# Scanning two sequences at a time in a Mamba-2 scan followed by a cosine-gated MLP

## The chip, the cores and the metric

The kernel runs on one core of one Trainium2 chip. The metric is the device time of one execution in microseconds. The engines of a core work from queues of their own, each in order: PE (TensorE; PEld is its weight load), DVE (VectorE), ACT (ScalarE), POOL (GpSimd), and SP, which here only issues DMAs. They wait for each other through semaphores.

## The reference

Part one is a scan over chunks. For 4 batches, 8 heads, 768 positions, head size 32 and state size 16 it computes, chunk by chunk:

```python
L = exp(cum[i] - cum[j]) * (i >= j)          # products of a from j+1 to i
M = (C @ B.T) * L
y = M @ x  +  (C @ state) * exp(cum)         # inside the chunk, and from the chunks before
state = exp(sum(la)) * state + sum_j(B_j x_j * exp(cum[-1] - cum[j]))
```

Part two takes y as a (3072, 256) matrix: `h = y @ w_in` (256 to 2048), `g = h * cos(h)`, `out = g @ w_out` (2048 to 256). Everything is in fp32.

## The kernel before

The kernel scans chunks of 128 positions, so there are NC = 6 of them; a "sequence" b is one of the 4 batches with all its 8 heads. Part two runs in 96 steps, 16 for each chunk, numbered n. The loop over n at the end of the code sets the order on every engine: the code is written out in the order in which each engine's queue shall hold it, and nothing reorders it.

A step n has these pieces. `first(n)` computes a 128x512 piece of h in PSUM (tile hp, L462; two such banks take turns); ACT rounds it (k, L466), DVE takes the fraction of a turn (w, L468). `gate(n)` lets ACT take the sine (L473, it writes w in place) and DVE multiply it with hp (gT, L475). From chunk 1 on `differ(n)` lets POOL form differences of gT (gd, L500, L502, L503), since `second` there uses seven products in place of eight. `second(n-2)` multiplies gT and gd with w_out, or with sums of its blocks (tile words after `differ_w`, L494), into o (L518 in chunk 0, L556 after it). After every eighth step o is copied out and combined by four POOL additions (sum, L571).

The scan of a sequence of chunks 1 to 5 is spread over four steps in a row. `reaches` and the first half of `decays` come first: scans on DVE which give the running product of a along the chunk (reach, L333) and the decays of four heads (lam, L342). Then `turn` (with the second half of decays): PE transposes B and C into tp (L355, L356), ACT copies them to cT and bcT (L360, L362) and DVE writes C times reach (L364). Then `intra`: four matmuls on strips of 32 rows give g (L374), DVE multiplies it with lam (m, L387). Then `finish`: y is summed from the state (L397) and from m (L406), ACT copies it to yT (L411), `sum_up` gives the chunk's share of the state (s_ps, L423) and `carry` renews the state (whole on DVE, L438, state on POOL, L441). The tiles tp, g, y and s_ps take turns in two PSUM buffers of two banks each ("scan"). Sequences 0 to 3 of a chunk start at the steps 6, 10, 14 and 18 of the chunk before.

In chunk 0 there is one more job. The weights come from DRAM in 16 pieces (words) and are rounded in place: `grade` (ACT L193 and L191, POOL L194) and `join` (DVE L207 and L209, POOL L217). Piece n is graded and joined in step n, the join behind gT. The clipped a is written to DRAM (a_cut, a_all, L637) and read back broadcast over the partitions (arow, along) for the scans.

The loop's end, where the four steps of a sequence stand:

```python
            if j == 0:
                reaches(c, b)
                decays(c, b, 0)
            elif j < 4:
                (turn, intra, finish)[j - 1](c, b)
                if j == 1:
                    decays(c, b, 1)
```

Of the kernel before, what the change touches and what calls it, by code (L numbers as in the profile page):

```python
# [25 lines left out]
def kernel(  # L26
# [50 lines left out]
    states = ctx.enter_context(tc.tile_pool(name="states", bufs=NB + 1))  # L77
# [252 lines left out]
    def reaches(c, b):  # L330

        reach[c, b] = r = scan.tile([P, P], FP32, tag="reach", bufs=2, name="reach")
        V.tensor_tensor_scan(out=r, data0=along[c][:, b], data1=ones, initial=1.0,  # L333
                             op0=ALU.mult, op1=ALU.mult)
# [16 lines left out]
    def turn(c, b, tag=None):  # L351
        bc = raw[c][0]
        tp = (pair("tp")[:, 0] if tag is None else bank([P, 4 * P], "tp", tag)
              ).rearrange("p (k i) -> p k i", k=4)
        PE.transpose(tp[:, 0], bc[:, 0, heads(b)].rearrange("p h n -> p (h n)"), ident)  # L355
        PE.transpose(tp[:, 1], bc[:, 1, heads(b)].rearrange("p h n -> p (h n)"), ident)  # L356
# [4 lines left out]
        bcT = scan.tile([P, 2, P], FP32, tag="bcT", name="bcT")  # L361
        ACT.copy(out=bcT[:, 0], in_=tp[:, 0])  # L362
        if c > 0:
            V.tensor_tensor(out=bcT[:, 1], in0=tp[:, 1], in1=reach[c, b], op=ALU.mult)  # L364
        part[c, b] = (bcT, cT)

    def intra(c, b):
        bcT, cT = part[c, b]
        g = [pair("g") for _ in range(2)]
        for u in range(4):  # L370
            r = slice(32 * u, 32 * u + 32)
            rhs = (cT[r].rearrange("p t i -> p (t i)") if c > 0 else
                   cT[r].rearrange("p t (s i) -> p s t i", s=2))
            PE.matmul(g[u // 2][:, u % 2, 0:2 * P], lhsT=bcT[r, 0], rhs=rhs,  # L374
                      start=True, stop=True)
        l = lam.pop((c, b))
        m = scan.tile([P, H, P] if c > 0 else [P, 2, H, W], FP32, tag="m", name="m")

        def of(t, u):
            hs = slice(u * HH, (u + 1) * HH)  # L380
            return (t[:, hs].rearrange("p (k t) i -> p k (t i)", k=2) if c > 0 else
                    t[:, :, hs].rearrange("p s (k t) i -> p k s (t i)", k=2))
        for u in range(2):
            in0 = g[u][:, :, 0:2 * P]
            if c == 0:
                in0 = in0.rearrange("p k (s i) -> p k s i", s=2)
            V.tensor_tensor(out=of(m, u), in0=in0, in1=of(l, u), op=ALU.mult)  # L387
        part[c, b] = (bcT, m)

    def finish(c, b, tag=None, fills=0):  # L390
        (bcT, m), xr = part.pop((c, b)), raw[c][1]
        if c > 0:

            y = pair("y")[:, :, 0:P]
            for q in range(4):
                r, p = slice(32 * q, 32 * q + 32), 64 * (q % 2)
                PE.matmul(y[p:p + 64, q // 2], lhsT=state[c - 1, b][r].rearrange("p t d -> p (t d)"),  # L397
                          rhs=bcT[r, 1], start=True, stop=False, tile_position=(32 * q, p),
                          skip_group_check=True)
        else:  # L400
            y = bank([P, 4, P], "y", tag)
            fill(y[:, 2:4], fills)
            y = y[:, 0:2]
        for h in range(H):
            q, t = h % 4, h // 4
            PE.matmul(y[32 * q:32 * q + 32, t], lhsT=xr[:, b, h], rhs=m[:, h] if c > 0 else m[:, :, h],  # L406
                      start=(c == 0 and t == 0), stop=True, tile_position=(0, 32 * q),
                      skip_group_check=True)
        if b == 0:
            yT[c] = two.tile([P, 2, TB], FP32, tag="yT", name="yT")  # L410
        ACT.copy(out=yT[c][:, :, b * P:(b + 1) * P], in_=y)  # L411
# [323 lines left out]
```

## Time and profile before

| | |
|---|---|
| median of 3 runs | 397.01 us (396.37 to 397.31) |
| the profiled execution's own time | 395.98 us |
| its span, first to last instruction | 394.2 us |
| PE busy | 385.5 us (98%) |
| DVE, ACT, POOL busy | 258.3, 178.4, 248.5 us (66%, 45%, 63%) |
| mean granted TensorE clock | 0.994 |

The time is the span and 1.8 us around it. The busy share of PE counts matmuls that wait in the array as work, so the 98% does not say that PE runs at its best. The trace counts every matmul as two rows, since it is run in two passes: four matmuls of the code are "x8". Line numbers of the profile are those of the kernel before; those of the changed kernel are named with the changed names.

### The profile page before, as it was taken

To read this page: it belongs to the slowest core of one execution; us is meant where nothing else is said; L and a number is where in the kernel's file an instruction comes from. 1 tells how busy PE (TensorE), PEld (TensorE's weight loads), DVE (VectorE), ACT (ScalarE), POOL (GpSimd) and SP (SyncE) were. 2 spreads that over 40 slices of the span, in tenths; PEclk is the share of its full clock that TensorE was granted. 3 is DMA by queue.
4 is the path that set the end of the run, shared out by engine and by line. 5 is a ranking of instruction groups with operands and counts; after the bars stand their busy time and mean duration, and the time that the engine had idled before them with its cause. 6 is when DMAs were issued, how large, how long until landed. Compare 5 with 4: busy or idle time off the path is not lost.

```text
span 394.2 us, 7794 instructions
## 1 busy us (share of the span) xinstructions
PE 385.5 (98%) x2980; PEld 331.8 (84%) x2980; DVE 258.3 (66%) x408; ACT 178.4 (45%) x343; POOL 248.5 (63%) x373
## 2 busy tenths in 40 slices
PE   8989998999999999999999999999999999999996
PEld 2578876788899898898898998988988989889995
DVE  8877877587666765756756657648557656673443
ACT  4777664443444444344434434333434344444431
POOL 6665566638757657847846846857765755754651
PEclk9999999899999999999999999999999999999999
DMA  7969899709502309702206812122120000010011
GB/s 89 277 176 282 240 212 143 151 21 136 125 2 62 87 2 116 140 2 62 79 10 98 107 51 60 30 62 60 28 62 0 23 6 0 2 29 0 2 28 27
DMA packets 106373, 30.43 MB, mean 77 GB/s; under 512 B 75520, under 2 KB 102240, under 8 KB 106336
## 3 DMA queue, kind: packets, MB, share of 16 engines
q1 hardware_dynamic: 106176, 29.81, 37.2%
q8 instruction: 23, 0.38, 0.4%
q10 hardware_dynamic: 160, 0.13, 0.1%
q14 instruction: 14, 0.11, 0.1%
HBM read 26.59 MB, written 3.34 MB: 76 GB/s over the span
## 4 chain that ended last, share of the span: by engine, by line
PE 84%; DVE 6%; POOL 3%; DMA 2%; ACT 2%; SPq 1%; issue 1%; POOLq 0%; DVEq 0%
PE hp L462 38%; PE o L556 31%; PE g L374 3%; PE y L406 3%; PE y L397 2%; PE o L518 2%; DVE mag L209 2%; DMA words<-in_moe_w_out_dram 1%; DMA arow<-a_cut 1%; POOL w_in L217 1%; DVE mag L207 1%; DVE lam L342 1%; ACT w L473 1%; PE a_ps L298 1%; DVE w L468 1%
## 5 line engine op out<-in xcount | busy, mean ns | idle before, releaser
L462 PE MATMUL hp<-yT,w_in 128*128 128x256 f32 x768 | 187.5, 387 | 0.3 <-POOL w_in L217 0.2
L462 PEld LDWEIGHTS hp<-yT,w_in 128*128 128x128 f32 x768 | 139.5, 191 | 26.0 <-issue 7.4
L500 POOL TENSOR_TENSOR gd<-gT 128x256 f32<-128x256 f32 x79 | 79.7, 1008 | 90.3 <-DVE gT L475 84.6
L475 DVE TENSOR_TENSOR gT<-hp,w 128x512 f32<-128x512 f32 x96 | 66.4, 692 | 81.5 <-ACT w L473 79.4
L473 ACT ACTIVATE w<-w,quarter 128x512 f32<-128x512 f32 x96 | 69.3, 722 | 105.0 <-DVE w L468 105.0
L466 ACT ACTIVATE k<-hp 128x512 int32<-128x512 f32 x96 | 57.4, 598 | 94.0 <-PE hp L462 94.0
L468 DVE SCALAR_TENSOR_TENSOR w<-hp,k 128x512 f32<-128x512 f32 x96 | 65.1, 679 | 43.9 <-ACT k L466 43.9
L556 PE MATMUL o<-words,gd 128*128 128x128 f32 x474 | 65.8, 275 | 0.0
L556 PEld LDWEIGHTS o<-words,gd 128*128 128x128 f32 x474 | 59.3, 192 | 0.0
L342 DVE TENSOR_TENSOR_SCAN lam<-arow,unit 128x512 f32<-128x512 f32 x40 | 56.2, 1404 | 0.0
L556 PEld LDWEIGHTS o<-w_out,gT 128*128 128x128 f32 x316 | 47.6, 191 | 4.0
L502 POOL TENSOR_TENSOR gd<-gT,gd 128x128 f32<-128x128 f32 x79 | 44.7, 566 | 6.2
L556 PE MATMUL o<-w_out,gT 128*128 128x128 f32 x316 | 48.0, 274 | 0.0
L503 POOL TENSOR_TENSOR gd<-gT,gd 128x128 f32<-128x128 f32 x79 | 35.9, 455 | 6.2
L387 DVE TENSOR_TENSOR m<-g,lam 128x512 f32<-128x512 f32 x48 | 30.7, 682 | 1.6 <-PE g L374 0.6
L518 PE MATMUL o<-w_out,gT 128*128 128x256 f32 x128 | 30.8, 384 | 1.0 <-POOL w_out L217 1.0
L556 PE MATMUL o<-words,gT 128*128 128x128 f32 x158 | 30.6, 275 | 0.0
L556 PE MATMUL o<-w_out,gd 128*128 128x128 f32 x158 | 30.5, 275 | 0.0
L518 PEld LDWEIGHTS o<-w_out,gT 128*128 128x128 f32 x128 | 24.7, 194 | 4.9 <-POOL w_out L217 1.4
L556 PEld LDWEIGHTS o<-words,gT 128*128 128x128 f32 x158 | 24.0, 192 | 0.0
L556 PEld LDWEIGHTS o<-w_out,gd 128*128 128x128 f32 x158 | 24.0, 192 | 0.0
L217 POOL TENSOR_TENSOR w_in<-mag,last 128x512 uint32<-128x512 uint32 (+1 forms) x9 | 12.3, 1368 | 13.0 <-DVE mag L209 9.2
(83 smaller groups left out, 308.4 us busy)
## 6 DMA issues: line engine op xcount, KB each, us to landing
arow<-a_cut SPq DMA_DIRECT2D x20, 512.0 KB
words<-in_moe_w_in_dram SPq DMA_DIRECT2D x8, 512.0 KB
words<-in_moe_w_out_dram SPq DMA_DIRECT2D x8, 512.0 KB
out_dram<-sum SPq DMA_DIRECT2D x18, 128.0 KB
xr<-in_x_dram SPq DMA_DIRECT2D x4, 512.0 KB
along<-a_all SPq DMA_DIRECT2D x20, 64.0 KB
xr<-in_x_dram SPq DMA_DIRECT2D x8, 128.0 KB
bc<-in_B_dram SPq DMA_DIRECT2D x4, 256.0 KB
```

The source lines that it names most:

```text
L342: V.tensor_tensor_scan(out=lam[c, b][:, hs].rearrange("p h i -> p (h i)"), data0=rows_.rearrange("p h i -> p (h i)"), data1=unit.rearrange ...
L387: V.tensor_tensor(out=of(m, u), in0=in0, in1=of(l, u), op=ALU.mult)
L462: PE.matmul(to_[:, e], lhsT=w_in[:, k, fs], rhs=y[:, k, u], start=(k == 0), stop=(k == KT - 1), skip_group_check=True)
L466: ACT.activation(k, hp[n], AF.Copy, bias=0.25, scale=INV_2PI)
L468: V.scalar_tensor_tensor(out=w, in0=hp[n], scalar=INV_2PI, in1=k, op0=ALU.mult, op1=ALU.subtract)
L473: ACT.activation(cos, cos, AF.Sin, bias=quarter, scale=TWO_PI)
L475: V.tensor_tensor(out=gT[n], in0=hp.pop(n), in1=cos, op=ALU.mult)
L500: G.tensor_tensor(out=d[:, 0:2], in0=g[:, 1:2].to_broadcast([P, 2, P]), in1=g[:, 3::-3], op=ALU.subtract)
L502: G.tensor_tensor(out=d[:, 2], in0=g[:, 0], in1=d[:, 0], op=ALU.subtract)
L503: G.tensor_tensor(out=d[:, 3], in0=g[:, 2], in1=d[:, 2], op=ALU.subtract)
L518: PE.matmul(o[c, u][:, t], lhsT=g[:, 2 * e + t], rhs=w_out[:, 2 * j + e], start=(j == e == t == 0), stop=(j == NJ - 1 and e == 1), skip_gr ...
L556: PE.matmul(at[q], lhsT=a_[q], rhs=w[q], start=(j == 0 and q in starts), stop=(j == NJ - 1), skip_group_check=True)
```

## The change

In chunks 1 to 5 two sequences (a pair, u = 0 or 1) are scanned together: `turn2` transposes both, `intra2` forms g of both, `masked` multiplies with lam one sequence in each of two steps, and `finish2` sums y from both states, then from both m, then both sums. Pair u starts (`turn2`) at step 11 (u = 0) or 19 (u = 1) for chunk 1, and 16 steps later for each chunk after it; g stands one step later, finish2 three steps later. The four halves of decays stand in the four steps ahead of turn2, one in each, and both reaches in the last of these; for the first pair of chunk 1 the halves stand at the steps 4, 6, 8 and 9. `turn2` stands ahead of the sine in its step.

In chunk 0 a piece is graded one step ahead from step 2 on, and from step 3 on the join stands between w and gT. The differences of w_out are made two at a time at the steps 14, 15, 17 and 19. The clip of a is on POOL for both copies and stands ahead of the first join. One more short matmul on ones stands at the start, the third transpose of chunk 0 stands ahead of the second `cross`, and the buffers of states, sum and reach are changed.

```diff
+    def turn2(c, u):
+        tp = pair("tp")[:, 0].rearrange("p (s k i) -> p s k i", s=2, k=2)
+        for s in range(2):
+            for k in range(2):
+                PE.transpose(tp[:, s, k], bc[:, k, heads(2 * u + s)]..., ident)
+        bT = scan.tile([P, 2, P], FP32, tag="bT2", bufs=1, name="bT2")
+        ACT.copy(out=bT, in_=tp[:, :, 0])
+        cT = scan.tile([P, 2, 2, P], FP32, tag="cT2", bufs=1, name="cT2")
+        for t in range(2):
+            ACT.activation(cT[:, :, t], tp[:, :, 1], AF.Copy, scale=slot[:, t:t + 1])
+        rT = scan.tile([P, 2, P], FP32, tag="rT", bufs=1, name="rT")
+        V.tensor_tensor(out=rT, in0=tp[:, :, 1], in1=reach[c, u], op=ALU.mult)
+    def intra2(c, u):
+        g = [pair("g") for _ in range(2)]
+        for s in range(2):
+            for q in range(4):
+                r = slice(32 * q, 32 * q + 32)
+                PE.matmul(g[q // 2][:, q % 2, s * 2 * P:(s + 1) * 2 * P], lhsT=bT[r, s],
+                          rhs=cT[r, s]..., start=True, stop=True)
...
-    V.tensor_scalar(out=la, in0=a_in, **clip)
     cut = const.tile([RB, NU, P], FP32, name="cut")
     G.tensor_scalar(out=cut, in0=a_in, **clip)
     G.memset(cut[:, :, 0:1], 0.0)
+    G.tensor_scalar(out=la, in0=a_in, **clip)
...
+    join("in", 0)
+    finish(2, "o")
+    intra(3)
...
-    differ_at = {NF - 7: (0, fore), NF - 6: (1, fore), NF - 5: (2, fore), NF - 4: (3, fore),
-                 NF - 1: (0, hind), NF: (1, hind), NF + 1: (2, hind), NF + 2: (3, hind)}
+    differ_at = {NF - 2: [(0, fore), (1, fore)], NF - 1: [(2, fore), (3, fore)],
+                 NF + 1: [(0, hind), (1, hind)], NF + 3: [(2, hind), (3, hind)]}
+    TURN = (NF - 5, NF + 3)
...
+            for at in pairs(n):
+                turn2(*at)
+            rests = [grade(*piece[m], later=True) for m in ... if m in piece]
             gate(n)
...
+            if not early and n in piece:
+                join(*piece[n])
+            gated(n)
...
         if n >= LAG:
             second(n - LAG)
+        for c, u in pairs(n - 1):
+            intra2(c, u)
+            masked(c, 2 * u)
+        for c, u in pairs(n - 2):
+            masked(c, 2 * u + 1)
+        for c, u in pairs(n - 3):
+            finish2(c, u)
+        for c, b, t in halves_at(n):
+            decays(c, b, t)
+        for c, u in pairs(n + 1):
+            for b in (2 * u, 2 * u + 1):
+                reaches(c, b)
```

Three places in the built order. On PE, the scan of sequence 0 of chunk 1, from its transposes to its sums (hp and o are part two). Before:

```order
L355 MATMUL tp<-ident,bc 128x128
L356 MATMUL tp<-ident,bc 128x128
L462 MATMUL hp<-yT,w_in 128x256 x4
L518 MATMUL o<-w_out,gT 128x256 x4
L374 MATMUL g<-cT,bcT 128x256 x4
L462 MATMUL hp<-yT,w_in 128x256 x4
L518 MATMUL o<-w_out,gT 128x256 x4
L397 MATMUL y<-bcT,state 64x128 x4
L406 MATMUL y<-m,xr 32x128 x8
L423 MATMUL s_ps<-xr,sc 32x64 x4
```

The same place now, for sequences 0 and 1:

```order
L405 MATMUL tp<-ident,bc 128x128 x4
L571 MATMUL o<-w_out,gT 128x256 x4
L512 MATMUL hp<-yT,w_in 128x256 x4
L571 MATMUL o<-w_out,gT 128x256 x4
L422 MATMUL g<-cT_724,bT_722 128x256 x8
L512 MATMUL hp<-yT,w_in 128x256 x4
L571 MATMUL o<-w_out,gT 128x256 x4
L512 MATMUL hp<-yT,w_in 128x256 x4
L571 MATMUL o<-w_out,gT 128x256 x4
L447 MATMUL y<-rT,state 64x128 x8
L454 MATMUL y<-m,xr 32x128 x16
L471 MATMUL s_ps<-xr,sc 32x64 x8
```

Each group of the scan holds twice the matmuls, so PE goes from part two to the scan and back half as often; a step more lies between g and y.

On ACT, the turn of sequence 1 of chunk 1 before (w is the sine, mag and last are the grading):

```order
L466 ACTIVATE k<-hp 128x512
L193 ACTIVATE mag<-words 128x512
L473 ACTIVATE w<-w,quarter 128x512
L191 ACTIVATE last<-words 128x512
L360 ACTIVATE cT<-tp,slot 128x128 x2
L362 COPY bcT<-tp 128x128
L466 ACTIVATE k<-hp 128x512
```

The turn of the first pair now:

```order
L516 ACTIVATE k<-hp 128x512
L408 COPY bT_722<-tp 128x256
L411 ACTIVATE cT_724<-tp,slot 128x2x128 x2
L193 ACTIVATE mag<-words 128x512
L523 ACTIVATE w<-w,quarter 128x512
L191 ACTIVATE last<-words 128x512
L516 ACTIVATE k<-hp 128x512
```

The copies of the transposes no longer stand behind the sine.

On DVE, steps of chunk 1 in which the next scans are made. Before:

```order
L468 SCALAR_TENSOR_TENSOR w<-hp,k 128x512
L475 TENSOR_TENSOR gT<-hp,w 128x512
L333 SCALAR_TENSOR_TENSOR reach<-along,ones 128x128
L342 SCALAR_TENSOR_TENSOR lam<-arow,unit 128x512
L468 SCALAR_TENSOR_TENSOR w<-hp,k 128x512
L475 TENSOR_TENSOR gT<-hp,w 128x512
L364 TENSOR_TENSOR bcT<-tp,reach 128x128
L342 SCALAR_TENSOR_TENSOR lam<-arow,unit 128x512
L468 SCALAR_TENSOR_TENSOR w<-hp,k 128x512
L475 TENSOR_TENSOR gT<-hp,w 128x512
L387 TENSOR_TENSOR m<-g,lam 128x512 x2
L468 SCALAR_TENSOR_TENSOR w<-hp,k 128x512
```

Now (ps is the copy of o after every eighth step):

```order
L518 SCALAR_TENSOR_TENSOR w<-hp,k 128x512
L528 TENSOR_TENSOR gT<-hp,w 128x512
L344 SCALAR_TENSOR_TENSOR lam<-arow,unit 128x512
L518 SCALAR_TENSOR_TENSOR w<-hp,k 128x512
L528 TENSOR_TENSOR gT<-hp,w 128x512
L619 COPY ps<-o 128x512
L344 SCALAR_TENSOR_TENSOR lam<-arow,unit 128x512
L518 SCALAR_TENSOR_TENSOR w<-hp,k 128x512
L528 TENSOR_TENSOR gT<-hp,w 128x512
L344 SCALAR_TENSOR_TENSOR lam<-arow,unit 128x512
L335 SCALAR_TENSOR_TENSOR reach<-along,ones 128x128 x2
L518 SCALAR_TENSOR_TENSOR w<-hp,k 128x512
```

The scans of lam, which came in two of every four steps, now come in four steps in a row and then not for four; the copy ps lies among them, and both reaches stand behind the last.

More of the change, by code (lines that the diff above doesn't have):

```diff
@@ L399, in finish @@
                           skip_group_check=True)
[L400 to L409, printed above, removed]
-            yT[c] = two.tile([P, 2, TB], FP32, tag="yT", name="yT")
@@ L411, in finish @@
-        ACT.copy(out=yT[c][:, :, b * P:(b + 1) * P], in_=y)
-        if 0 < c < NC - 1:
-            sum_up(c, b, pair("s_ps")[:, 0, 0:2 * D])
-            carry(c, b)
-    sums = {}
+        for s in range(2):
+            for h in range(H):
+                q, t = h % 4, h // 4
+                PE.matmul(y[32 * q:32 * q + 32, t, s * P:(s + 1) * P], lhsT=xr[:, 2 * u + s, h],
+                          rhs=ms[s][:, h], start=False, stop=True, tile_position=(0, 32 * q),
+                          skip_group_check=True)
@@ L605 @@
     fill(warm, 2)
+    fill(warm[:, 0:2])
     spread_a(0, "h")
-    turn(0, 0)
+    turn(0)
     spread_a(1, "h")
```

215 lines of the change are left out of this document (125 added, 90 removed).

## The prediction, made before the changed kernel was run

> **What bounds the kernel now.** I read the page's chain of work that ended last, then the granted clock and busy time by stretches, then PE's timeline of a steady stretch and of every place where PE stood still.
>
> ```profile
> PE 84%; DVE 6%; POOL 3%; DMA 2%; ACT 2%; SPq 1%; issue 1%; POOLq 0%; DVEq 0%
> ...
> 49.20:65.40 16.20, 15.62 (x102) 12.90 (x98) 12.03 (x19) 7.96 (x14) 11.04 (x12) 1.00 0.97 191
> 68.90:72.30 3.40, 3.40 (x9) 2.69 (x8) 1.40 (x3) 1.83 (x3) 3.15 (x4) 0.50 1.28 168
> 75.00:385.00 310.00, 309.96 (x2493) 276.27 (x2490) 196.77 (x299) 130.82 (x248) 199.56 (x306) 1.00 0.26 48
> ```
>
> The columns of the last three lines are the stretch and its length, busy time of PE, PEld, DVE, ACT and POOL, the granted clock, DMA. From 75 us to 385 PE never stops (309.96 of 310.00); there only what PE itself spends counts, as long as DVE (63%) and POOL (64%) keep up. Before 75 PE has waits, and once the clock is halved for 3.4 us.
>
> What PE spends there on one sequence of the scan (chain first, then timeline; start, length):
>
> ```profile
> 141.24 1.73 PE hp L462 x8
> 142.97 1.56 PE o L556 x14
> ```
>
> ```profile
> 144.36 0.27 PE L355 MATMUL tp<-ident,bc 128*128 128x128 f32 x1
> ...
> 144.58 1.89 PE L462 MATMUL hp<-yT,w_in 128*128 128x256 f32 x8
> 146.31 0.61 PE L556 MATMUL o<-w_out,gT 128*128 128x128 f32 x4
> ...
> 147.97 0.71 PE L374 MATMUL g<-cT,bcT 32*128 32x256 f32 x8
> 148.61 1.99 PE L462 MATMUL hp<-yT,w_in 128*128 128x256 f32 x8
> 150.44 0.61 PE L556 MATMUL o<-w_out,gT 128*128 128x128 f32 x4
> ...
> 152.09 0.45 PE L397 MATMUL y<-bcT,state 32*64 32x128 f32 x8
> 152.47 0.64 PE L406 MATMUL y<-m,xr 128*32 128x128 f32 x16
> 152.93 0.29 PE L423 MATMUL s_ps<-xr,sc 128*32 128x64 f32 x8
> 153.16 0.48 PE L462 MATMUL hp<-yT,w_in 128*128 128x256 f32 x1
> ```
>
> A step of part two is 1.73 + 1.56 = 3.29 us, so 256 columns stream in 1.73 / 8 = 0.216 us. The transposes take 144.58 - 144.36 = 0.22 and cost nothing at either side. The g group: o from 146.31 would be through at 147.87, g starts at 147.97 (0.10 lost), hp follows at 148.61 (0.64), and this hp takes 150.44 - 148.61 = 1.83 where 1.73 is usual (0.10 lost): 0.84 together. Four strips run side by side, so the streaming in it is two passes, 0.43; 0.41 is switching. The y group in the same way: 152.00 to 153.16, and 0.10 in the hp behind: 1.26. Its streams are 0.22 (L397, two passes of 128 columns), 0.43 (L406, four) and 0.11 (L423, two of 64): 0.76. So 0.50 is switching.
>
> **Term 1, the scan in pairs: -9.0 us.** A pair has the streams of two sequences and, if the second sequence's matmuls follow without a gap, the switching of one: it saves 0.41 + 0.50 = 0.9 us. There are 10 pairs (the last two without s_ps, which hardly touches the switching): 9.0. The transposes save nothing. All of it lies on the path where PE never stops; the first pair saves it only if PE is the bound there too (term 2). Bounds: a gain of 9.4 if the start of y on a second state is hidden as well, and 6.0 if the second sequence's weights show.
>
> On this last point there is a row, of the weight loads of the g group above:
>
> ```profile
> 147.96 0.31 PEld L374 LDWEIGHTS g<-cT,bcT 32*128 32x128 f32 x8
> ```
>
> All eight loads are done at 148.27, the matmuls go on to 148.68: the second pass, on the same four strips of rows, finds its weights loaded while the first streams. I count nothing for the loads. The Trainium skill says otherwise ("TensorE: Matmul & The Clock Gate", Part 3, The mechanism): a weight load overlaps matmuls in flight only when its row group differs. By that rule the second sequence, which uses the same strips again, would show its loads; the trace speaks against it, and what it would cost is the rival "loads show" below.
>
> **Term 2, the waits of PE between 53 and 74 us: -4.8 us.**
>
> ```profile
> 53.51 0.45 PE L397 MATMUL y<-bcT,state 32*64 32x128 f32 x8 [0.58 <-DVE m L387]
> ...
> 63.53 1.89 PE L518 MATMUL o<-w_out,gT 128*128 128x256 f32 x8
> 66.98 1.45 PE L374 MATMUL g<-cT,bcT 32*128 32x256 f32 x8 [1.57 <-ACT bcT L362]
> 68.37 3.29 PE L462 MATMUL hp<-yT,w_in 128*128 128x256 f32 x8
> 71.45 2.33 PE L518 MATMUL o<-w_out,gT 128*128 128x256 f32 x8
> 73.89 0.45 PE L397 MATMUL y<-bcT,state 32*64 32x128 f32 x8
> ```
>
> ```profile
> 64.97 0.72 ACT L473 ACTIVATE w<-w,quarter 128x512 f32<-128x512 f32 x1 [3.70 <-DVE w L468]
> ...
> 66.67 0.26 ACT L362 COPY bcT<-tp 128x128 f32<-128x128 f32 x1
> ```
>
> ```profile
> 60.70 0.43 DVE L207 TENSOR_SCALAR mag<-mag 128x512 uint32<-128x512 uint32 x1 [1.24 <-POOL mag L194]
> ...
> 62.11 2.25 DVE L342 TENSOR_TENSOR_SCAN lam<-arow,unit 128x512 f32<-128x512 f32 x1
> ```
>
> ```profile
> 58.56 1.28 POOL L494 TENSOR_TENSOR words<-w_out 128x512 f32<-128x512 f32 x1
> ```
>
> The story reads backwards: g waits 1.57 for bcT; bcT stands on ACT behind the sine of its step, which waited 3.70 for w; w stands on DVE behind lam (2.25) and a join that waited 1.24 for POOL's mag; mag stands on POOL behind a difference of w_out. From 63.53 to 73.89 PE spends 10.36, where o, g, hp and o with the 0.09 ahead of y come to 1.73 + 0.84 + 1.83 + 1.73 + 0.09 = 6.22 at full rate: 4.1 lost, 1.7 of them by half the clock over 3.4 us. With the 0.58 at 53.51, and 0.1 for the m that y still waited for: 4.8. The change takes each link away: the turn stands ahead of the sine, mag is made a step earlier, the differences wait until step 14, and no join is left behind gT to delay a scan. What is late next is DVE in the steps 8 to 11, with join and scan or reaches in each, and POOL at 17 to 19, with two differences beside gd. DVE was busy 12.03 of 16.20 us in the stretch from 49.2, so it can catch up; I price both at **+0.5** (bounds 0, and 3.4 if a wait as long as the old one comes back with its lower clock).
>
> On the clock, a row and a rule differ: the trace halves it for 3.4 us right after a stop of 1.57. The Trainium skill (same page, "Why this matters for your kernels") warns only of idle gaps over about 3 us; by it the old stop would have cost 1.7 less, but the trace decides.
>
> **Term 3, the start: -0.5 us.**
>
> ```profile
> 25.64 1.99 PE L518 MATMUL o<-w_out,gT 128*128 128x256 f32 x8 [0.97 <-POOL w_out L217]
> ```
>
> ```profile
> 16.58 0.73 POOL L217 TENSOR_TENSOR w_in<-mag,last 128x256 uint32<-128x256 uint32 x1 [1.28 <-DVE mag L209]
> ...
> 21.74 0.40 POOL L634 TENSOR_SCALAR cut<-a_in 96x256 f32<-96x256 f32 x1
> ...
> 22.38 0.61 POOL L194 TENSOR_SCALAR mag<-mag 128x512 f32<-128x512 f32 x1
> ```
>
> ```profile
> SPq L637 <- POOL cut L635: 6.9, 1, 6.9
> ```
>
> The first o waits for POOL's w_out, whose mag (22.38) stands behind the clip (21.74): 0.6 goes from this chain. The clips move into POOL's wait of 1.28 ahead of 16.58, where two of 0.40 and a memset fit. The extra matmul on ones may give 0.1 back; so -0.5 (bounds -0.9 and +0.5). SP, which stood 6.9 us at a_cut with all later loads queued behind it, goes on that much earlier: this has to carry the pieces that ACT now grades a step (3.5 us) earlier. I take it as covered, at 0; if a piece came a microsecond late, the sine behind it would, and gT has slack (next term).
>
> **Term 4, POOL in the steady stretch: +2.4 us.**
>
> ```profile
> 146.84 1.21 DVE L342 TENSOR_TENSOR_SCAN lam<-arow,unit 128x512 f32<-128x512 f32 x1
> ...
> 157.43 0.69 DVE L475 TENSOR_TENSOR gT<-hp,w 128x512 f32<-128x512 f32 x1 [0.86 <-ACT w L473]
> ```
>
> ```profile
> 146.87 1.71 POOL L500 TENSOR_TENSOR gd<-gT 128x256 f32<-128x256 f32 x1 [1.49 <-DVE gT L475]
> ...
> 149.19 0.45 POOL L503 TENSOR_TENSOR gd<-gT,gd 128x128 f32<-128x128 f32 x1
> 149.60 0.41 POOL L327 TENSOR_TENSOR sc<-bc,lam 128x128 f32<-128x128 f32 x1
> ...
> 155.47 0.72 POOL L571 TENSOR_TENSOR sum<-ps 128x256 f32<-128x256 f32 x1
> 156.27 1.94 POOL L571 TENSOR_TENSOR sum<-ps,sum 128x256 f32<-128x256 f32 x3
> ```
>
> A lam that starts first holds POOL up: gd's first part takes 1.71 there, and the step's three parts 149.64 - 146.87 = 2.8. Now lam stands in four steps in a row, straight behind gT: POOL needs 4 x 2.8 = 11.1, two sc 0.8, and the four sums, which fall into the third of these steps (the order shows ps there), 2.7: 14.6 against 4 x 3.29 = 13.2 of PE, so it falls 1.4 behind, and more where reaches holds it. Its slack: gT ends at 158.12, 4.9 after its hp (153.26 without the lost 0.10); the second part of gd, which PE wants first, is there 2.3 later, at 7.2; PE asks at 6.58 + 1.73 + 0.45 = 8.8 after the hp. So 1.6 of slack against 1.4 and more: I take a wait of 0.3 for gd in each of the 8 pairs that follow step 20, 2.4. Bounds: 0, and 0.9 a pair, which would eat term 1 (8). DVE alone is no bound there: gT may be 6.58 - 4.9 = 1.7 late before the next hp but one wants its bank, and a lam of 1.21 fits behind it.
>
> **The sum.** -9.0 - 4.8 + 0.5 - 0.5 + 2.4 = -11.4. The profiled execution took 395.98, so it would take 384.6; the median of the runs shown is 1.0 higher, so the forecast is 385.6.
>
> **Rivals.** (a) POOL keeps up and nothing new waits in chunk 0: 385.6 - 2.9 = 382.7. For it: 199.56 of 310 us are all POOL does; against: it comes in lumps. (b) The waits between 53 and 74 come back in another place, DVE at the steps 8 to 11 for instance, with the clock: 385.6 + 4.8 = 390.4. For it: the stretch has the densest queues. (c) Loads show: two more loads of about 0.10 (what the hp behind a switch loses) in g and one in y for a pair, 0.3 x 10: 388.6. Only the rule quoted speaks for it. (d) Slower: DVE's scans become the bound. Where POOL is first, lam takes 2.25 (row at 62.11). If POOL, late by its lumps, is always in the middle of something when lam starts, four such scans cost 4 x 1.04 = 4.2 and the two reaches (a quarter of a lam's elements each, so at 0.4 an estimate from the 1.21) another 0.8 in four steps; less the slack of gT (1.7) and of the transposes of two sequences (0.4), PE would stop 2.9 us for each of 8 pairs, 23 us against the 14.3 of terms 1 to 3: 406. It decides from a mean lam of about 2.0 in these steps; now the one straight behind a short multiply is 1.21. (e) The change saves nothing net, because each pair waits 0.9 for gd and the waits of chunk 0 stay: 397.
>
> **Chances.** Forecast 0.51, (a) 0.20, (b) 0.14, (c) 0.05, (d) 0.06, (e) 0.04. The forecast, (a), (b) and (c) are all faster by more than 0.2% (about what a measurement here can tell from no change): 0.90; same 0.04; slower 0.06. The range runs from (a) with bounds taken kindly, 381.5, to a little past (b), 391.0; (d) and (e) lie outside.
>
> **What would show it.** Right: in the timeline a g group of 16 rows of about 1.07 us up to the next hp; no stop over 0.5 and a clock of 1.00 between 45 and 75; eight steady steps in about 30.4 us where they took 31.0. Term 4: among the waits, PEld of o on POOL gd, 0.3 each, in the step behind turn2. Wrong: if lam's mean rises over 1.7, if ACT waits for words by DMA, or if the g group takes over 1.2.

## The result, and the profile after

| | before | changed |
|---|---|---|
| median | 397.00 us (4 runs, 396.37 to 397.31) | 385.72 us (4 runs, 385.63 to 386.67) |
| ratio | | 0.9723, 95% interval 0.9704 to 0.9743 |
| profiled execution, and its span | 395.98, 394.2 us | 386.67, 384.9 us |

The forecast was 385.6 us. The two profiled executions lie 9.3 us apart and the medians 11.3: the profile of before is 1.0 below its median and that of the changed kernel 0.95 above (it is the slowest of its four runs). The section on the prediction says what part of that the traces explain.

First the two views on which the prediction was built, for the changed kernel: the chain by engine, then the stretches (start and end, length, busy time of PE, PEld, DVE, ACT and POOL, granted clock, DMA).

```profile
PE 82%; DVE 7%; POOL 3%; ACT 2%; issue 2%; DMA 2%; SPq 1%; ACTq 0%
```

```profile
49.20:65.40 16.20, 15.96 (x86) 13.10 (x86) 16.03 (x24) 10.74 (x20) 10.03 (x10) 1.00 1.07 184
68.90:72.30 3.40, 3.40 (x17) 2.73 (x15) 2.79 (x5) 1.84 (x4) 0.27 (x1) 1.00 1.14 272
75.00:375.00 300.00, 299.38 (x2468) 272.07 (x2467) 196.37 (x282) 122.41 (x206) 197.74 (x300) 1.00 0.26 48
```

The half clock from 68.9 is gone, and PE stands still for 0.24 us between 49.2 and 65.4, where it lost 0.58. DVE is now busy there for 16.03 of 16.20 us (12.03 before), so it has no room left in this stretch. From 75 us on PE loses 0.62 us in 300, where it lost 0.04 in 310. The waits say where (engine and line, what it waited for, us in total, times, longest):

```profile
PE o L609 <- POOL gd L555: 0.6, 1, 0.6
PE hp L512 <- DVE gT L528: 0.2, 1, 0.2
...
PEld o L609 <- POOL gd L555: 2.2, 9, 0.8
```

A steady pair, in the chain (start, length, what). This is the answer to the rows that the prediction measured for one sequence:

```profile
124.41 1.81 PE o L609 x14
126.22 1.08 PE g L422 x16
127.30 1.92 PE hp L512 x8
...
134.07 0.59 PE y L447 x16
134.67 1.01 PE y L454 x32
135.68 0.22 PE s_ps L471 x16
```

g of two sequences takes 1.08, where one took 0.64, with 0.10 lost on either side of each such group. The o ahead of it takes 1.81 in place of 1.56: this is the wait for gd, 0.25, once in each pair.

Where the time went is read from the starts of hp, the first matmul of each step (rows of L462 and L512 in PE's timeline, in us from the start of the span; "alone" is the experiment that changes chunk 0 only, "later halves" the one that moves the scans, both below):

| start of step | before | changed | difference | later halves | alone |
|---|---|---|---|---|---|
| 0 | 17.36 | 18.80 | +1.44 | 18.34 | 18.38 |
| 3 | 27.48 | 28.38 | +0.90 | 27.92 | 28.50 |
| 8 | 44.96 | 45.74 | +0.78 | 45.30 | 46.09 |
| 16 | 82.19 | 77.71 | -4.48 | 77.26 | 78.37 |
| 24 | 113.63 | 108.92 | -4.71 | 107.64 | 109.65 |
| 32 | 144.58 | 139.22 | -5.36 | 137.70 | 140.61 |
| 88 | 360.58 | 351.26 | -9.32 | 347.63 | 356.64 |
| end | 394.20 | 384.88 | -9.32 | 381.23 | 390.25 |

The start loses 0.9, the steps 8 to 16 gain 5.3 (one pair in them), the second pair gains almost nothing (steps 16 to 24: 0.23), and each of the other eight pairs about 0.6: eight steady steps take 139.22 - 108.92 = 30.30 us where they took 30.95.

### The profile page after: what moved, and what is told of

The parts are those of the page before. It is cut to its first block, busy times and chain, and to the rows that moved or that the text cites. A ratio compares the mean times of both kernels' runs of the same rounds, so it can differ in the third digit from the quotient of the medians.

```text
span 384.9 us, 7726 instructions
## 1 busy us (share of the span) xinstructions
PE 378.3 (98%) x2982; PEld 331.2 (86%) x2982; DVE 265.9 (69%) x395; ACT 172.9 (45%) x303; POOL 245.4 (64%) x366
## 4 chain that ended last, share of the span: by engine, by line
PE 82%; DVE 7%; POOL 3%; ACT 2%; issue 2%; DMA 2%; SPq 1%; ACTq 0%
PE hp L512 37%; PE o L609 32%; PE g L422 3%; PE y L454 3%; DVE mag L209 2%; DVE w L518 2%; DMA xr<-in_x_dram 2%; PE y L447 2%; DVE lam L344 2%; PE o L571 1%; DVE gT L528 1%; PE warm L101 1%; ACT w L523 1%; PE a_ps L298 1%; PE tp L405 1%
## 5 line engine op out<-in xcount | busy, mean ns | idle before, releaser
L512 PE MATMUL hp<-yT,w_in 128*128 128x256 f32 x768 | 184.4, 383 | 0.6 <-POOL w_in L217 0.3
L512 PEld LDWEIGHTS hp<-yT,w_in 128*128 128x128 f32 x768 | 139.2, 190 | 22.7 <-issue 4.5
L553 POOL TENSOR_TENSOR gd<-gT 128x256 f32<-128x256 f32 x79 | 71.9, 911 | 89.5 <-DVE gT L528 86.2
L518 DVE SCALAR_TENSOR_TENSOR w<-hp,k 128x512 f32<-128x512 f32 x96 | 65.4, 681 | 36.7 <-ACT k L516 36.4
L609 PE MATMUL o<-words,gd 128*128 128x128 f32 x474 | 67.0, 277 | 0.6 <-POOL gd L555 0.6
L344 DVE TENSOR_TENSOR_SCAN lam<-arow,unit 128x512 f32<-128x512 f32 x40 | 55.7, 1394 | 0.0
L609 PEld LDWEIGHTS o<-w_out,gT 128*128 128x128 f32 x316 | 46.9, 191 | 3.6
L555 POOL TENSOR_TENSOR gd<-gT,gd 128x128 f32<-128x128 f32 x79 | 43.1, 546 | 6.2
L556 POOL TENSOR_TENSOR gd<-gT,gd 128x128 f32<-128x128 f32 x79 | 35.9, 455 | 6.2
L571 PEld LDWEIGHTS o<-w_out,gT 128*128 128x128 f32 x128 | 24.2, 190 | 4.0 <-POOL w_out L217 0.8
L435 DVE TENSOR_TENSOR m<-g,lam 128x512 f32<-128x512 f32 x40 | 25.6, 681 | 0.0
L624 POOL TENSOR_TENSOR sum<-ps,sum 128x256 f32<-128x256 f32 (+1 forms) x27 | 24.2, 909 | 1.4
```

The source lines that it names most:

```text
L344: V.tensor_tensor_scan(out=lam[c, b][:, hs].rearrange("p h i -> p (h i)"), data0=rows_.rearrange("p h i -> p (h i)"), data1=unit.rearrange ...
L435: V.tensor_tensor(out=of[0], in0=g[q][:, :, s * 2 * P:(s + 1) * 2 * P], in1=of[1], op=ALU.mult)
L512: PE.matmul(to_[:, e], lhsT=w_in[:, k, fs], rhs=y[:, k, u], start=(k == 0), stop=(k == KT - 1), skip_group_check=True)
L518: V.scalar_tensor_tensor(out=w, in0=hp[n], scalar=INV_2PI, in1=k, op0=ALU.mult, op1=ALU.subtract)
L553: G.tensor_tensor(out=d[:, 0:2], in0=g[:, 1:2].to_broadcast([P, 2, P]), in1=g[:, 3::-3], op=ALU.subtract)
L555: G.tensor_tensor(out=d[:, 2], in0=g[:, 0], in1=d[:, 0], op=ALU.subtract)
```

## The experiments

All medians are of 4 or 5 runs; the kernel before ran with them at 396.75 to 397.02. The theory is the prediction's: switching on PE (0.41 in g and 0.50 in y for a pair) and the waits of chunk 0 make the gain, a wait for gd takes part of it back. The rival is that the pairs gain otherwise, by fewer instructions on DVE and ACT or by the moved turn.

**The scans away from the sums (term 4).**

```diff
-    halves_of = {u: [(t - 4 + i, 2 * u + i // 2, i % 2) for i in range(4)]
+    halves_of = {u: [(t - (5, 4, 3, 1)[i], 2 * u + i // 2, i % 2) for i in range(4)]
```

> The changed kernel with the four halves of lam 5, 4, 3 and 1 steps ahead of turn2 in place of 4, 3, 2 and 1, so that none stands in the step of the four sums. If PE's wait for gd in the step behind turn2 (0.25 us a pair, 8 pairs) comes from POOL being held up by lam in the step of its sums, as term 4 has it, the wait goes and the time falls by about 2.0 to 383.7. Rival: POOL is late by its sums alone; then the wait stays and the time is 385.7.

Measured 383.48 us (383.03 to 383.74), ratio to before 0.9663 (0.9649 to 0.9677): 2.24 faster than the changed kernel. PE waits for gd nowhere any more. POOL's timeline of the same step, of the changed kernel and then of this one (hp of the step starts at 122.52 and at 121.24):

```profile
118.02 1.25 POOL L555 TENSOR_TENSOR gd<-gT,gd 128x128 f32<-128x128 f32 x1
...
120.57 2.87 POOL L624 TENSOR_TENSOR sum<-ps,sum 128x256 f32<-128x256 f32 x3
...
124.33 0.46 POOL L555 TENSOR_TENSOR gd<-gT,gd 128x128 f32<-128x128 f32 x1
```

```profile
116.74 0.46 POOL L555 TENSOR_TENSOR gd<-gT,gd 128x128 f32<-128x128 f32 x1
...
118.50 2.86 POOL L624 TENSOR_TENSOR sum<-ps,sum 128x256 f32<-128x256 f32 x3
...
122.25 0.46 POOL L555 TENSOR_TENSOR gd<-gT,gd 128x128 f32<-128x128 f32 x1
```

The second part of gd takes 1.25 beside lam and 0.46 without it, so the whole row behind it comes 0.8 earlier: 1.01 after hp where it was 1.81. Eight steady steps, with one pair in them, take 30.06 us: 0.24 less than the changed kernel, and 0.89 less than the 30.95 of before, which is the 0.9 of term 1 with no wait against it. The second pair of chunk 1 gains 0.83 at step 20, where the changed kernel stood 0.6 to 0.8. By the edit three scans stand a step earlier, and the step of the sums holds none. Term 4 is shown, and the wait at step 20 goes with the same edit.

**g split (term 1).** On the kernel with the later halves, g of the first sequence stands behind hp and g of the second behind o, so PE goes to g and back twice in each pair.

```diff
+            for at in pairs(n - 1):
+                intra2(*at, (0,))
...
-            intra2(c, u)
+            intra2(c, u, (1,))
```

> The changed kernel with the later halves (the run before, 383.5 us), in which g of the two sequences is no longer formed in one go: g of the first stands behind hp, g of the second behind o of the same step, so that PE goes from part two to g and back twice for each pair, as in the kernel before; y and the sums stay joint. In the trace of the run before, bT, cT and rT are there before hp of this step ends, so no new wait is expected. If a switch to g and back costs the 0.41 us that the prediction reads (term 1), 10 pairs cost 4.1: 387.6 us, and a steady pair 0.41 more. If the gain of the change lies in the waits and in the fewer instructions of DVE and ACT and not in the switching, nothing: 383.5. If half of the switching hides behind the hp or o ahead: 385.5.

Measured 387.82 us (387.68 to 388.83), ratio 0.9778 (0.9761 to 0.9796): 4.34 more than the 383.48 of its base, where 4.1 was expected. The chain of a steady pair:

```profile
124.54 0.65 PE g L425 x8
125.19 1.76 PE o L613 x14
126.95 0.64 PE g L425 x8
127.59 1.92 PE hp L516 x8
```

Two groups are 1.29 against 1.08, and the o behind the first takes 1.76 where 1.56 is usual: 0.41 in all, and no wait stands there. Eight steps take 30.47, 0.41 more. The first two pairs cost more in the trace, 0.67 and 0.88, so that the median comes so near to ten times 0.41 is in part chance.

**y split (term 1).** The same for y, first with the first sequence behind hp of the old step.

```diff
+            for at in pairs(n - 3):
+                finish_y(*at, (0,))
...
-        for c, u in pairs(n - 3):
-            finish2(c, u)
+        for c, u in pairs(n - 3):
+            finish2(c, u)      # now the second sequence, and both sums
```

> The changed kernel with the later halves (383.5 us), in which y of the two sequences is no longer summed in one go: state and m of the first stand behind hp, those of the second and both sums behind o of the same step; g stays joint. If a switch to y and back costs the 0.50 us that the prediction reads (term 1), 10 pairs cost 5.0, and the split adds within y a second state group behind the first m group, as the kernel before had it: 388.5 us, a steady pair 0.50 more. With g split, the run before showed 0.41 more for each steady pair and 387.8, so the rival that a switch costs nothing is out for g; for y it would still give 383.5, and a first m that is not there in time 385 or more with a wait on DVE m.

Measured 392.92 us (392.56 to 393.84), ratio 0.9907 (0.9891 to 0.9923), 9.4 more than its base and far over the 388.5 of term 1. The third case expected, 385 or more with a wait for DVE's m, is what came: the edit brought a wait of its own, in each of the ten pairs.

```profile
134.04 0.45 PE L450 MATMUL y<-rT,state 32*64 32x128 f32 x8 [0.42 <-DVE m L435]
```

The m that the profile names is of the second sequence, and the y here reads only the first. By the code, y takes the buffer of the first half of g, and this m is its last reader. So 0.42 of the 0.98 that a pair took more was a wait. The split was therefore made once more, a step later: the first sequence at the old place behind o, the second and both sums behind the next step's hp.

> The split of y once more, on the changed kernel with the later halves (383.5 us), without the wait that the first split brought: there y of the first sequence, behind hp, waited 0.42 us for each pair (the profile names DVE's m: the buffer of g that y takes is read until then), and a steady pair took 0.98 more, 0.56 of it in the groups. Now state and m of the first sequence stand at the old place of y (behind o), those of the second and both sums behind the next step's hp, where all m are there. By term 1 (0.50 a pair): a steady pair 0.50 to 0.56 more and no wait of y, 388.5 to 389. If the switch costs nothing and the first split lost by its wait alone and by what that drags along: 383.5 to 384.

Measured 388.20 us (388.07 to 389.00), ratio 0.9786 (0.9770 to 0.9802): 4.7 more than its base, with no wait of y.

```profile
133.72 0.38 PE y L450 x8
134.10 0.57 PE y L456 x16
134.67 1.93 PE hp L520 x8
136.60 0.38 PE y L450 x8
136.97 0.57 PE y L456 x16
...
137.77 1.76 PE o L617 x14
```

Eight steps take 139.37 - 108.82 = 30.55 us against 30.06: 0.49 for a pair, by the rows 0.38 + 0.57 twice against 0.60 + 1.01 (0.29 more) and 0.20 in the matmul group behind. The two splits together undo 0.41 + 0.49 = 0.90 for a pair. That is term 1, and the rival that the pairs gain otherwise is out.

**Only what belongs to chunk 0 (term 2).** The kernel before, with the turn of one sequence ahead of the sine, grading a step ahead, the join ahead of gT and the late differences; no pairs, the start and the clip as before.

```diff
             first(n)
+            turn(c, b)            # at its old step, was behind second(n - 2)
-            rest = grade(*piece[n], later=True)
+            rests = [grade(*piece[m], later=True) for m in ...]    # n + 1 from n = 2 on
             gate(n)
+            join(*piece[n])       # from n = 3 on; was behind gated(n)
             gated(n)
```

> The kernel before, with only what term 2 speaks of: turn (of one sequence, at its old step) ahead of the sine, pieces graded a step ahead from step 2 on, joins between w and gT from step 3 on, the differences of w_out two at a time at the steps 14, 15, 17 and 19. No pairs, the scans of DVE, the start and the clip as before. If the waits between 53 and 74 us go by this alone (term 2: 4.8, less the new waits): 392 to 393, with no stop over 0.5 and no half clock there. If they go only because the scans come in another pattern (halves earlier for the first pair): 396 to 397, with the wait of g on bcT still there. In steady steps the turn ahead of the sine changes nothing by the prediction, since bcT has a step's slack there: 30.96 us for 8 steps.

Measured 392.18 us (391.43 to 392.44), ratio 0.9881 (0.9865 to 0.9896): 4.60 less than before, where term 2 with its new waits says 4.3. PE's busy time and the clock in the stretch:

```profile
45.00:75.00 30.00, 30.00 (x202) 24.57 (x201) 26.72 (x43) 18.08 (x36) 13.14 (x16) 1.00 1.05 208
```

No stop is left there, though every scan stands at its old step; the rival, that the waits go only because the scans come in another pattern, is out. In its steady stretch nothing changes: from step 18 to the end it stays 3.9 to 4.0 ahead of before, so for single sequences the place of the turn is worth nothing there.

**The parts of chunk 0, undone in the changed kernel.** All three at once (grading at its own step, join behind gT, single differences at the old steps):

```diff
-    differ_at = {NF - 2: [(0, fore), (1, fore)], ...
+    differ_at = {NF - 7: [(0, fore)], NF - 6: [(1, fore)], ...
-    EARLY = 3
+    EARLY = NC * NF
-                     for m in ((n,) if early else ()) + ((n + 1,) if n >= EARLY - 1 else ())
+                     for m in ((n,) if early else ()) + ()
```

> The changed kernel with chunk 0's extra work in the old order: each piece graded in its own step, joined behind gT, the differences of w_out one at a time at the old steps 9 to 12 and 15 to 18; the pairs stay. Term 2 says that these orders took away most of 4.8 us of waits between 53 and 74 us: the time rises by 3 to 5, to about 389.5, with a wait of PE over 1 us and half the clock behind it. Rival: the new places of the scans (halves at the steps 4, 6, 8, 9, one turn at 11) took the waits away by themselves; then the time stays within 1 us of 385.7.

Measured 389.20 us (389.02 to 389.34), ratio 0.9808 (0.9793 to 0.9823): 3.5 more. Part of the old waits is back, PE's o now waiting for w_out; the half clock that was expected behind it did not come.

```profile
63.50 1.99 PE L571 MATMUL o<-w_out,gT 128*128 128x256 f32 x8 [1.43 <-POOL w_out L217]
...
75.28 0.67 PE L447 MATMUL y<-rT,state 32*64 32x128 f32 x16 [0.55 <-DVE m L435]
```

POOL's timeline ahead of the first of them shows the link that the prediction named, a difference of w_out (words) in front of mag:

```profile
58.62 1.28 POOL L547 TENSOR_TENSOR words<-w_out 128x512 f32<-128x512 f32 x1
...
60.24 0.61 POOL L194 TENSOR_SCALAR mag<-mag 128x512 f32<-128x512 f32 x1
```

Then two of the three by themselves: the join back behind gT, and the differences back at their old steps.

> The changed kernel with one thing undone: the join of a piece stands behind gT on DVE from step 3 on, as before the change; pieces are still graded a step ahead and the differences of w_out made late. With the grading at its own step, the old join and the old differences together the kernel took 389.2 (3.5 more than the changed one). If the join's place is what matters (it delays the scans behind gT): 387.5 or more. If the grading a step ahead is (mag is there in time in any case): 386.0. Steady steps as in the changed kernel.

Measured 387.66 us (386.66 to 387.85), ratio 0.9764 (0.9746 to 0.9782): 1.9 more than the changed kernel. The chain that ends in y of the first pair lies on DVE almost throughout, where a join stands behind gT in each step, and y waits:

```profile
73.62 0.67 PE L447 MATMUL y<-rT,state 32*64 32x128 f32 x16 [0.33 <-DVE m L435]
```

> The changed kernel with one thing undone: the differences of w_out stand singly at the steps 9 to 12 and 15 to 18, as before the change. If they are what holds mag (POOL) and so the join and the scans up: 387 to 388, with waits of PE at the steps 10 to 15; and the wait for gd behind step 20 (0.8) should be gone or smaller, since no two of them stand at step 19. If the grading a step ahead gives enough room for them: 385 to 385.7, that is same or a little faster by the 0.8 at step 20.

Measured 386.78 us (386.03 to 387.16), ratio 0.9744 (0.9727 to 0.9762): 1.1 more, though the two intervals overlap. The trace shows two new waits, and in turn the wait for gd behind step 20 is gone (the way from step 20 to 21 takes 0.83 less, as expected):

```profile
60.95 1.97 PE L512 MATMUL hp<-yT,w_in 128*128 128x256 f32 x8 [0.48 <-DVE gT L528]
...
66.17 1.99 PE L512 MATMUL hp<-yT,w_in 128*128 128x256 f32 x8 [0.45 <-DVE gT L528]
```

The starts differ by up to a microsecond between executions (next section), so the parts are better read from the traces, counted from the start of step 0. At step 16 all three undone cost 3.83, the join's place 1.27 and the differences 0.94; 1.6 is left for the grading a step ahead, which was not undone by itself, and for what the three do to each other. Some of it is given back later: at the end the three cost 2.9, the join's place 0.65 and the differences 0.10, since their 0.94 is paid back by the 0.83 at step 20. So it is not shown that the old differences make the kernel slower. In the two kernels with the join behind gT the time is 2.1 to 2.2 us more than the span, where it is 1.8 in the changed kernel; that is part of the 3.5 and the 1.9 above, and no view shows where it comes from.

**The turn behind the sine.** The changed kernel with `turn2` where `turn` stood.

```diff
-            for at in pairs(n):
-                turn2(*at)
             rests = ...
             gate(n)
...
             gated(n)
+            for at in pairs(n):
+                turn2(*at)
```

> The changed kernel with turn2 behind the sine and gT of its step, as the old turn stood behind the sine. If the place on ACT was a link of the old wait, g of the first pair of chunk 1 waits for bT2 on ACT again and the time rises by 0.5 to 2; in the steady stretch DVE's rT behind gT costs nothing. Rival: with joins ahead of gT and grading a step ahead the sine is no longer late, and the place of the turn is worth nothing: 385.7.

Measured 392.02 us (391.47 to 392.82), ratio 0.9886 (0.9867 to 0.9905): 6.3 more than the changed kernel, a miss of the expectation by a wide margin. The loss is 1.36 at step 12 and 1.2 at step 20, and then 0.4 in each steady pair, where nothing was expected. ACT's timeline of a steady pair, then DVE's, and PE's chain behind them:

```profile
125.92 0.72 ACT L523 ACTIVATE w<-w,quarter 128x512 f32<-128x512 f32 x1 [2.96 <-DVE w L518]
...
126.80 0.84 ACT L411 ACTIVATE cT<-tp,slot 128x256 f32<-128x256 f32 x2
```

```profile
127.67 0.42 DVE L413 TENSOR_TENSOR rT<-tp,reach 128x256 f32<-128x256 f32 x1 [0.23 <-ACT cT L411]
```

```profile
127.80 1.48 PE g L422 x16
```

DVE makes lam and both reaches ahead of w in just this step, so the sine waits 2.96 and the copies stand behind it. On DVE, rT waits for cT and ends at 128.10. By the code, half of g takes the buffer of tp, which rT reads: in the trace the first two matmuls of g start at 127.73, right behind cT, and the next at 128.15, behind rT. So g takes 1.48 in place of 1.08. The expectation had said that rT behind gT costs nothing.

**The start (term 3).** The extra matmul on ones taken out, first of the changed kernel, then of the one with the later halves.

```diff
     fill(warm, 2)
-    fill(warm[:, 0:2])
```

> The changed kernel without the one more short matmul on ones at the start. If that matmul lies on the path (its two passes of 256 columns at half clock are 0.85 us, and in the trace of the changed kernel the first a_ps starts at 5.62 us where it started at 4.44), the first h step starts about 0.8 us earlier and the time falls to about 384.9. If it hides behind a0s, or if it pays by bringing the clock up earlier, the time stays at 385.7 or rises.

> The changed kernel with the later halves (383.5) and without the extra matmul on ones at the start. Alone, the matmul left out changed nothing in the time (385.88 against 385.72), though hp of step 0 came 0.3 earlier; if that was given back in a wait that the later halves take away: 383.1. If the start is bound elsewhere: 383.5.

Measured 385.88 us (385.28 to 386.35), ratio 0.9724 (0.9707 to 0.9741), and 382.83 us (382.47 to 383.37), ratio 0.9648 (0.9632 to 0.9664). The first is no difference to the changed kernel, the second 0.65 less than its base, with ranges that overlap. What the matmul costs in time is not settled by the medians; the traces (next section) put it at 0.42 to 0.46 at the start. The second is the fastest kernel of the study.

The clip back at its old place, on the kernel with the later halves:

```diff
-    (cut, memset and la on POOL ahead of join("in", 0))
+    (la on DVE, cut and memset on POOL, behind join("in", 1))
```

> The changed kernel with the later halves (383.5 us), with the clip of a back at its old place: behind the joins of the first two pieces, one copy on DVE and the other on POOL. By term 3 it stands again in front of the mag for which the first o waits: hp of step 0 to hp of step 3 takes 0.54 to 0.6 more (10.1 in place of 9.58 us), and 0.5 in all if nothing gives it back: 384.0. If the shorter way there comes from the other edits of the start (the order of turns, grading): 383.5 and 9.6.

Measured 383.41 us (383.02 to 383.73), ratio 0.9662 (0.9648 to 0.9676), the same as its base. The wait is there, as among its waits of PE:

```profile
PE o L571 <- POOL w_out L217: 1.0, 1, 1.0
```

It was 0.4 with the clip moved, and from hp of step 0 to that of step 3 this kernel takes 28.31 - 18.18 = 10.13 us against 9.58. Of this 0.55, 0.14 is given back by step 12 in the trace, and nothing shows in the median.

## Why the prediction was right, and where it was not

**Term 1 (-9.0) held in size and in kind.** The splits cost 0.41 and 0.49 in the rows, and 4.3 and 4.7 in the medians of ten pairs: 9.1. A steady pair without a wait (the later halves) gains 0.89. The rival "loads show" is out: g of 16 rows takes 1.08, under the 1.2 named as its limit. The prediction set a rule of the Trainium skill against its row ("TensorE: Matmul & The Clock Gate", Part 3, The mechanism: a load overlaps matmuls in flight only when its row group differs, though the same section also lets loads into a background weight buffer go ahead); here the second sequence uses the same strips, and its loads cost nothing that can be seen: the loads of the group end at 126.89, its matmuls at 127.30.

```profile
126.15 0.74 PEld L422 LDWEIGHTS g<-cT,bT 32*128 32x128 f32 x16
```

What the prediction did not see is a condition of this term. It gave the place of the turn a worth in chunk 0 alone. With pairs the step of the turn is the step in which DVE is latest, and behind the sine the copies, with rT behind them, cost 0.4 in each steady pair, 3.2 us of term 1. Single sequences had no such loss.

**Term 2 (-4.8, +0.5 for new waits) held in size and in its links, but not in what it says of the clock.** By itself it measured -4.6 in the medians, and 4.97 in the traces counted from the start of step 0. The prediction's 6.22 us for the stretch at full rate counts 0.10 of hp twice (in the 0.84 and in the 1.83); it is 6.12, and 4.2 were lost. It puts 1.7 of this down to the half clock. The chain of the kernel before does not run through PE there:

```profile
69.83 1.27 POOL words L494
...
71.47 0.59 POOL mag L194
...
72.55 0.69 DVE mag L209
73.24 0.61 DVE m L387
...
73.89 0.45 PE y L397 x8
```

POOL works without a gap from 67.63 to 72.05, the join waits for its mag, m stands behind the join, and y waits for m. At the full rate PE would have reached y sooner and stood there longer. So the loss up to this y is these waits, and the half clock cost nothing on the path. The timed runs fit: of the 34 executions of the kernel before beside the experiments, 27 have a mean granted clock of 0.999 or 1.000, while 3.4 us at half rate would give 0.996; they take 396.28 to 397.43 us, and the seven with 0.994 or 0.995 no more than 396.30.

In the trace of the changed kernel the steps 7 to 16 gain 5.5, of which the first pair's switching is 0.9: 4.6, and the new wait there is the 0.24 for gT. The other new waits were sized at too little: "POOL at 17 to 19, with two differences beside gd" came as the chain says (start, length):

```profile
89.77 3.37 POOL words L547 x2
...
94.03 0.46 POOL gd L555
...
94.53 1.38 PE o L609 x10
```

Two differences behind each other hold POOL for 3.37 us, about a step, and o waits 0.6 to 0.8 for gd. So the new waits are 0.24 and 0.83 (what the later halves gave back there), 1.1 in place of 0.5.

**Term 3 (-0.5) is where the working failed.** Its first part is right: from step 0 to step 3 the changed kernel is 0.54 shorter, where 0.6 was counted for the clip. But ahead of step 0 it is 1.44 later, and 0.1 was counted for the extra matmul. Two things are in the 1.44. One is no property of the change. The matmuls on ones and the first real ones, in PE's timeline: of before, of the kernel with chunk 0 alone, whose code is the same as that of before up to there, and of the one with the turn behind the sine, whose start is that of the changed kernel:

```profile
1.06 3.45 PE L101 MATMUL warm<-ones 128*128 128x512 f32 x4 [1.06 <-DVE ones L96]
4.44 1.08 PE L298 MATMUL a_ps<-a0s,those 128*64 128x512 f32 x4
```

```profile
1.06 3.78 PE L101 MATMUL warm<-ones 128*128 128x512 f32 x4 [1.06 <-DVE ones L96]
4.77 1.77 PE L298 MATMUL a_ps<-a0s,those 128*64 128x512 f32 x4
```

```profile
1.06 3.87 PE L101 MATMUL warm<-ones 128*128 128x512 f32 x6 [1.06 <-DVE ones L96]
4.86 1.08 PE L298 MATMUL a_ps<-a0s,those 128*64 128x512 f32 x4
```

The same rows of a_ps take 1.08 in one execution and 1.77 in another: PE starts at half its rate (in the traces the matmuls on ones start 0.85 us apart, where their 512 columns stream in 0.43 later on) and comes to the full one at a moment that the code does not set. The clock records of the traces give this moment: 4.05, 6.20 and 4.02 us in these three executions, and 6.07 in that of the changed kernel. With the same code, hp of step 0 starts at 17.36 and at 18.38, 1.02 apart. The second thing is the extra matmul: in the first and the last pair of rows the moment is nearly the same, and there a_ps starts 0.42 and hp of step 0 0.46 later (17.82 against 17.36). With a late moment it is much the same: 18.38 without the matmul (moment at 6.08, the later halves without it) and 18.80 with it (6.07, the changed kernel). So the matmul on ones costs 0.42 to 0.46 on the path, not 0.1, and term 3 is about -0.1. The profiles differ by +0.9 at step 3 only because that of before had an early moment and that of the changed kernel a late one. The Trainium skill describes such a moment ("TensorE: Matmul & The Clock Gate", Part 1, What's actually happening): a window that runs freely and is not reset by a kernel's start. The rows agree, with 1.0 us between executions. The start alone moved by up to 1.24 us between executions of one and the same start (17.82 to 19.06 for hp of step 0, with the moment at 4.02 and at 6.59). That would carry the 2.0 us between profiles and medians if the timed runs fell the other way. Their mean clocks on record point that way: the profile of before (0.994, 395.98 us) is like the shortest of its executions, while 24 of the 34 timed ones beside the experiments have 1.000 and take 396.59 to 397.43; of the changed kernel the profiled one has 1.000 and 386.67, the other three 0.999 and 385.63 to 385.75. The timed runs left no trace, so that the start makes this difference is not shown.

**Term 4 (+2.4) held, and its reason too.** The wait is 0.25 a pair where 0.3 was taken, in the step and on the engine named, and it goes when the scan moves away from the sums: 8 pairs make 2.0, and with the 0.83 at step 20 it is 2.8; the median moved by 2.24, and the two traces by 3.7, of which 0.5 is their starts. Rival (a), that POOL keeps up, is what the later halves made: its 382.7 against 383.48 measured. Rivals (b), (d) and (e) are out: the clock stayed at 1.00, and lam's mean is 1394 ns, under the 1.7 and the 2.0 that were named.

```profile
L344 DVE TENSOR_TENSOR_SCAN lam<-arow,unit 128x512 f32<-128x512 f32 x40 | 55.7, 1394 | 0.0
```

The sign that the loads come late did not show: ACT waits for no words by DMA (the kernel before did once, for 0.7 us).

The sum by measured parts: -9.1 (both splits) - 4.6 (chunk 0 alone) - 0.1 (start, from the traces) + 2.2 (later halves) = -11.6, against -11.3 in the medians. The forecast was close because its large terms were right; the 0.4 too much at the start, the waits at step 20 and the 0.05 a pair too much for gd are of the size of the interval (0.4% of 397 us is 1.5). That it met the median to 0.1 us is luck. For the profiled execution it said 384.6, and that took 386.67; and with the 0.98 of the moment taken out (1.44 less the matmul's 0.46) the two traces lie 10.3 apart, not 11.4.

## What to carry to other kernels

Where PE never waits, count the switches between shapes of matmul: price one by what its group takes beyond its streams, in the group and in the one behind it, and halve their number by grouping. Then look at what the grouping bunches on the other engines: here four scans in a row met the four sums of POOL, and moving three scans a step earlier, away from the sums, brought 2.2 us; a copy that stands behind an instruction that waits for the latest engine has to be moved in front of it first. Before you count a half clock or a slow row as a loss, see whether the chain that releases the next instruction runs through it. Before you read a difference of a microsecond between two traces, compare their first rows: the start of PE alone may hold it.

## What the runs showed of the hardware

- With the same code ahead of it, the first step starts 1.02 us apart in two executions, by the moment at which PE reaches its full rate. Over the 14 traces this moment lies between 4.02 and 6.59 us. The column of the granted clock says 1.00 from the start on, since there is no record ahead of the moment; the lengths of the rows show it (a_ps 1.08 against 1.77).
- A stop of PE of 1.57 us (65.4 to 67.0) was followed by half clock from 68.9 to 72.3 in the profile of the kernel before; a stop of 1.43 us was followed by none (the kernel with the old chunk 0), and by their mean clock 27 of 34 timed executions of the kernel before had none either. In each of the 14 traces the time at full rate up to the next half clock is a whole number of times 3.413 us (in that of before 64.85, 19 times, and then one such time at half). So the clock seems to be judged once in 3.413 us, and how a stop falls on these points may decide; no run tests this.
- A second weight load on the same strips of rows is hidden for g (16 loads done 0.41 us ahead of the matmuls), so a group of two sequences has no cost beyond its streams and one switch.
- POOL's short product takes 0.46 us alone and 1.25 beside a scan on DVE that started first; that 0.8, in the queue ahead of the four sums, is what PE's wait of 0.25 came from.
